# Attention values with the exps as the stationary operand, a ones column for the sums, and x normalised by tokens

## Chip, cores, metric

The kernel runs on one core of one Trainium2 chip. The metric is device time in microseconds (us). A profiled execution gives the span between its first and last instruction, some 3 us (before) below the timed runs. A run is slow when it is over 1.5% above the fastest of the same kernel. The records also give the granted TensorE clock, as a share of full speed, over time.

## The reference, cut to what matters

```python
# q: (8, 16, 384, 64); k, v: (8, 4, 384, 64); four q heads share one k/v head
scores = scale * q @ k.T;  attn = exp(scores - max) / sum;  o = attn @ v
x = o.transpose(0, 2, 1, 3).reshape(8, 384, 1024)          # tokens x (heads * 64)
h = relu(x @ w_in)                                         # 1024 x 1024
u, vv = h[..., :512], h[..., 512:]
vn = (vv - mean(vv)) / sqrt(var(vv) + 1e-6)                # over the 512 features
vs = einsum('ts,bsd->btd', w_spatial, vn) + b_spatial      # mixes the 384 tokens
return (u * vs) @ w_out                                    # 512 x 1024
```

I call the eight batch entries images. Each has 384 tokens in three tiles (t) of 128. The 16 query heads form two groups (gp) of eight, that is, two k/v heads ("half") with four query heads (j) each.

## The kernel before

The program is a hand-written order. Short words stand for steps: `s` a pair of score matmuls, `e` their exps, `m` sums, `r` reciprocal, `x` values, `n` norm, `V` the v half of w_in, `U` the u half, `A` and `H` their first four of eight contraction tiles, `p` spatial, `O` projection. A prime means one image earlier, a plus one image later. Words with `l` load, `c` cast to 16 bits, `t` turn by DMA; `wv` and `wu` load the v and the u half of w_in (index 0: its first four row tiles, 1: its last four), `ws`, `cws`, `tws` load, cast and turn the spatial weights. The steps are played into one queue per engine, and a step that waits holds up what stands behind it in its queue.

The parts that the change touches:

```python
def tiles(dst, quad, streams):                 # four 32-column tiles of the array side by side
    for t, (weights, a) in enumerate(streams):
        for i in range(4):
            half, j = i // 2, quad * 2 + i % 2
            nc.tensor.matmul(dst[32 * i : 32 * (i + 1), :], weights[...],      # 32 stationary columns
                             a[:, half, j * S : (j + 1) * S], ...)             # 384 exps stream
def sums(b, gp, quad):   ...  tiles(f32(x, S), quad, [(ones32, a) for a in parts])
def recip(b, gp, quad):  nc.scalar.activation(rec, sums, AF.Ln); nc.scalar.activation(rec, rec, AF.Exp, scale=-1.0)
def value(b, gp, quad, jj): ... tiles(f32(x, S), quad, [(v16[..., 32 * jj : 32 * (jj + 1)], aT[:, t]) for t in range(NST)])
def norm(b, gp, quad, jj):
    nc.vector.tensor_tensor(T["xT", b][:, gp * 4 + quad * 2 + jj, :], f32(x, S), rec, ALU.mult)
...
def load_w_in(gp, c0, c1):                     # issued by GpSimd, four DMAs of 32 partitions
    for i in range(4): nc.gpsimd.dma_start(w_in16[32 * i : 32 * (i + 1), gp * 4 : gp * 4 + 4, c0:c1], ...)
...
RAMP1 = """ w28 cqjv00 ... w7 cqp011 wv0 cqv010 s0 e0 ... s7 e7
    cv wu0 lk+ lq0+ lq1+ lv+ ws ck+ lk++ cq0+ lq0++ wv1
    s8 m00 r00 x000 n000 ...
    cq1+ wu1 cv+ cws wo ck++ cq0++ m10 ... tws lv++ tk++ tq0++ lq1++ ... """
```

The result of the values stands transposed (features on partitions) and is at once what the feed-forward part needs. VectorE adds the exps of token tiles (`add`, `add2`) to make fewer sums matmuls necessary.

The softmax here doesn't subtract the row's maximum and nothing guards it: scores larger than these inputs give would overflow.

## Time and profile before

| | before |
|---|---|
| time, median of 2 | 252.81 us |
| span of the profiled run | 249.7 us |
| TensorE, VectorE, ScalarE, GpSimd busy | 238.1, 193.9, 172.3, 58.7 us |
| granted clock | 1.00 |

Busy time of TensorE is not work: records of pipelined matmuls overlap (a 512-column matmul of the v half is 380 ns long in the records, and such matmuls start 216 ns apart). What can be read is the distance between starts, and the prediction prices the work by it. Where TensorE never waits, the number of matmuls times that distance is the time.

### The profile page before, as it was taken

Reading aid. Unit: us, or ns where it says so; the run is one execution under the profiler, and the core shown is the slowest. Engines: PE = TensorE matmul, PEld = TensorE weight load, DVE = VectorE, ACT = ScalarE, POOL = GpSimd, SP = SyncE. Lnnn points to the kernel's source line nnn. Section 1 sums busy time; section 2 is a strip of 40 time slices with the busy share of each in tenths; the row PEclk is TensorE's granted clock in tenths of the full one; section 3 lists DMA queues with packets and bytes.
Section 4 is the critical chain, followed back from the end, with each engine's and each line's share of the span. In section 5 each row is a group of like instructions: output and inputs, shape, how many; then the busy total and the mean of one; then the engine's idle time right before and its main releaser. Section 6 shows DMA issues by size and latency. Waiting matters only on the chain.

```text
span 249.7 us, 6046 instructions
## 1 busy us (share of the span) xinstructions
PE 238.1 (95%) x2496; PEld 116.4 (47%) x2496; DVE 193.9 (78%) x365; ACT 172.3 (69%) x229; POOL 58.7 (23%) x100
## 2 busy tenths in 40 slices
PE   7689988989999999999999999999999999999993
PEld 6344434434455444444355444554354444554671
DVE  2626389896979869787979879786979679798853
ACT  3898899987794978677785978677884968430000
POOL 1927960123505400153006400371000000000000
PEclk9999999999999999999999999999999999999999
DMA  6999999749999375967099445959170202110424
GB/s 208 264 270 360 243 200 210 162 90 314 218 295 314 104 83 138 295 181 181 8 253 333 125 76 142 310 161 165 38 213 0 87 0 117 54 59 29 158 97 168
DMA packets 57227, 41.97 MB, mean 168 GB/s; under 512 B 26352, under 2 KB 53360, under 8 KB 57200
## 3 DMA queue, kind: packets, MB, share of 16 engines
q1 hardware_dynamic: 53936, 38.12, 58.2%
q0 software_dynamic: 2848, 3.15, 7.4%
q8 instruction: 19, 0.31, 0.5%
q10 hardware_dynamic: 416, 0.33, 0.4%
q14 instruction: 8, 0.07, 0.1%
HBM read 25.95 MB, written 12.58 MB: 154 GB/s over the span
## 4 chain that ended last, share of the span: by engine, by line
PE 69%; DVE 12%; ACT 12%; issue 3%; DMA 2%; DVEq 0%
PE banks L121 48%; PE banks L337 11%; PE banks L315 10%; ACT aT L327 9%; DVE xT L407 3%; DVE gT L525 2%; DVE sT L350 2%; ACT rec L376 1%; DMA q<-in_q_dram 1%; DVE vs L512 1%; ACT rec L374 1%; DVE bn L467 1%; DMA out_dram<-osb 1%; DVE v_r L456 1%; PE banks L288 1%
## 5 line engine op out<-in xcount | busy, mean ns | idle before, releaser
L327 ACT ACTIVATE aT<-banks 128x1024 f16<-128x1024 f32 x144 | 136.8, 1024 | 33.7 <-PE banks L315 33.5
L315 PE MATMUL banks<-qT,kT 64*128 64x512 f16 x288 | 44.3, 380 | 3.7 <-ACT aT L327 2.1
L121 PE MATMUL banks<-xT,w_in 128*128 128x384 f16 (+1 forms) x320 | 47.0, 294 | 0.6 <-DVE v_r L456 0.6
L121 PE MATMUL banks<-w_out,gT 128*32 128x512 f16 (+2 forms) x496 | 46.3, 379 | 1.3 <-DVE gT L525 0.8
L121 PE MATMUL banks<-w_in,xT 128*128 128x512 f16 x192 | 44.7, 380 | 0.3
L238 POOL CAST q<-q 128x384 f16<-128x384 f32 x57 | 32.2, 598 | 32.0 <-DMA q<-in_q_dram 31.5
L407 DVE TENSOR_TENSOR xT<-banks,rec 128x384 f16<-128x384 f32 x64 | 31.4, 551 | 9.3 <-ACT rec L376 9.2
L121 PEld LDWEIGHTS <-w_in 128*128 128x128 f16 x320 | 27.3, 98 | 16.0 <-issue 1.6
L337 PE MATMUL banks<-aT,v 128*32 128x384 f16 x768 | 34.4, 326 | 0.0
L545 DVE COPY osb<-banks 128x512 f32<-128x512 f32 x46 | 30.2, 683 | 5.4 <-PE banks L121 5.4
L121 PEld LDWEIGHTS <-gT 128*32 128x32 f16 (+1 forms) x496 | 18.4, 96 | 27.4 <-issue 7.2
L121 PEld LDWEIGHTS <-xT 128*128 128x128 f16 x192 | 17.5, 97 | 25.5 <-issue 7.1
L350 DVE TENSOR_TENSOR sT<-aT 128x1024 f16<-128x1024 f16 x39 | 28.1, 734 | 0.0
L337 PEld LDWEIGHTS <-v 128*32 128x32 f16 x768 | 20.6, 97 | 11.0 <-issue 1.2
L195 POOL CAST k<-k 128x768 f16<-128x768 f32 x7 | 6.6, 941 | 78.2 <-DMA k<-in_k_dram 78.2
L454 DVE TENSOR_SCALAR v_r<-banks 128x512 f32<-128x512 f32 x21 | 14.5, 692 | 13.3 <-PE banks L121 12.5
L315 PEld LDWEIGHTS <-kT 64*128 64x128 f16 x288 | 11.3, 94 | 28.6 <-issue 21.9
L374 ACT ACTIVATE rec<-banks 128x384 f32<-128x384 f32 x32 | 15.7, 490 | 8.2 <-PE banks L337 8.1
L121 PE MATMUL banks<-wsT,v_n 128*128 128x384 f16 x96 | 20.5, 327 | 0.1
L512 DVE TENSOR_TENSOR vs<-banks,bias_tp 128x384 f32<-128x384 f32 x28 | 15.3, 550 | 3.6 <-PE banks L121 3.6
L376 ACT ACTIVATE rec<-rec 128x384 f32<-128x384 f32 x32 | 16.7, 523 | 1.0
L467 DVE BATCH_NORM_STATS2 bn<-v_r 128x6 f32<-128x512 f32 x24 | 16.7, 694 | 0.8
(50 smaller groups left out, 144.4 us busy)
## 6 DMA issues: line engine op xcount, KB each, us to landing
q<-in_q_dram SPq DMA_DIRECT2D x31, 384.0 KB, 6.8
out_dram<-osb SPq DMA_DIRECT2D x22, 512.0 KB, 3.2
v<-in_v_dram SPq DMA_DIRECT2D x8, 384.0 KB, 6.9
k<-in_k_dram SPq DMA_DIRECT2D x7, 384.0 KB, 4.8
w_in<-in_moe_w_in_dram POOLq DMA_DIRECT2D x16, 128.0 KB, 6.9
w_out<-in_moe_w_out_dram POOLq DMA_DIRECT2D x2, 512.0 KB, 9.1
out_dram<-osb SPq DMA_DIRECT2D x3, 256.0 KB, 2.0
ws<-in_moe_w_spatial_dram SPq DMA_DIRECT2D x1, 576.0 KB, 9.0
```

The source lines that it names most:

```text
L121: nc.tensor.matmul(dst[c : c + cols], w[:, c : c + cols], m, start=(i == 0), stop=(i == n - 1))
L238: engine(T["q16", b, gp][:, 2 * qd : 2 * qd + 2, :, half, :], T["q32", b, gp][:, qd, 2 * half : 2 * half + 2, :].rearrange("p j (t d) -> p ...
L315: nc.tensor.matmul(banks[:, xs[half], :], T["kT", b][lo:hi, t, gp, :], rhs[lo:hi, c * 512 : (c + 1) * 512], start=True, stop=True,)
L327: nc.scalar.activation(T["aT", b, gp][:, t, :, c * 512 : (c + 1) * 512], banks[:, x : y + 1 : y - x, :], AF.Exp, scale=scale)
L337: nc.tensor.matmul(dst[32 * i : 32 * (i + 1), :], weights if len(weights.shape) == 2 else weights[:, half, :], a[:, half, j * S : (j + 1) ...
L350: engine.tensor_tensor(T["sT", b, gp][:, :, cs], aT[:, 0, :, cs], aT[:, 1, :, cs], ALU.add)
L374: nc.scalar.activation(rec, f32(x, S), AF.Ln)
L376: nc.scalar.activation(rec, rec, AF.Exp, scale=-1.0)
L407: nc.vector.tensor_tensor(T["xT", b][:, gp * 4 + quad * 2 + jj, :], f32(x, S), T["rec", b, gp, quad], ALU.mult)
L467: nc.vector.bn_stats(bn, T["v_r", b, st])
L512: nc.vector.tensor_tensor(vs, f32(x, S), bias_tp, ALU.add)
L545: copy(osb[:, half * 512 : (half + 1) * 512], banks[:, x, :])
```

## The change

The intent: make the exps the stationary operand and v the moving one. A matmul then gives 128 tokens by 64 features. With a ones column appended to v the 65th column is the sum, so the sums matmuls, the VectorE adds, and ScalarE's logarithm and exp for the reciprocal all go. The norm is then one product with a scalar per token and head. In return x stands with tokens on partitions and must be transposed for the feed-forward part. In steady images, two of three token tiles go through TensorE (`Tq`, with a VectorE copy) and one through the DMA (`T`). The whole order was rewritten too (`START`, `STEADY`; in it `X` and `N` are values and norm of one token tile, `Q`, `K` and `Tp` are transposes of q, k and x on TensorE), and w_in is loaded in two DMAs of 128 partitions per piece instead of four of 32.

```diff
-    def tiles(dst, quad, streams): ...      -    def add / add2 / sums / recip ...
+    def value(b, gp, tq):
+        xs = T["X", b, gp, tq] = take2()
+        for half in range(2):
+            for j in range(G):
+                col = column(b, gp, j, tq)
+                aT, o = T["aT", b, gp, col // 4], (col % 4) * P
+                for t in range(NST):
+                    nc.tensor.matmul(banks[:, xs[half], j * (D + 1) : (j + 1) * (D + 1)],
+                                     aT[:, t, half, o : o + P], T["v16", b][:, 2 * gp + half, t, :], ...)
+    def norm(b, gp, tq):
+        nc.vector.reciprocal(rec, ps[:, :, :, D : D + 1])
+        nc.vector.tensor_tensor(T["x16", b, tq][:, gp], ps[:, :, :, 0:D], rec.to_broadcast([P, 2, G, D]), ALU.mult)
+    def turn_x_dma(b, tq): nc.sync.dma_start_transpose(new_xT(b)[:, tq, :, :], ...)
+    def turn_x_all(b, tq, copy): ... 8 x nc.tensor.transpose(...); copy(xT[:, tq, :, :] ..., ps)
... (q by token tiles, load_w_in in two DMAs, the orders) ...
+    START = """ ... s4 wv0 e1 ws e0 wv1 s6 w5 s5 cqv110 lq0+ lv+ cv ckv1 s3 e4 e3 cqv101 ck+ s7 lq1+ K1
+        cq0+ cqv111 wu0 e5 e7 lq0++ lk++ s8 e6 cq1+ Q10 Q11 lq1++ ... s14 e12 cq0++ s16 ...
+        cv+ S1 X12 cws s0+ Q10+ ... s1+ Tp12 H0 wu1 wo e2+ tws V2 ck++ lv++ ... p0 U0 ... """
```

## The prediction

> **What bounds the kernel now.** I first read the engine totals, where TensorE stands out, and then asked whether "busy" means "working", because records of matmuls overlap. In the first fence the columns are busy time, share of the span and instruction count; in the second, the chain of work that ended last in one steady image, they are start, length (both us), what, and how many.
>
> ```profile
> PE 238.1 (95%) x2496; PEld 116.4 (47%) x2496; DVE 193.9 (78%) x365; ACT 172.3 (69%) x229; POOL 58.7 (23%) x100
> ```
>
> ```profile
> 206.60 0.96 PE banks L315 x6
> 207.57 1.84 PE banks L121 x32
> 209.41 2.60 PE banks L337 x64
> 212.01 0.76 PE banks L315 x6
> ```
>
> The chain stays on TensorE here, so the distance between starts is the price of an instruction. 64 column-tiled matmuls of L337 (32 output rows, 384 columns) cost 2.60 us: 40.6 ns each. Six scores run as three concurrent pairs; 0.76 us is three times 216 ns (the start-to-start distance of 512-column matmuls in the trace) and about 0.1 us more. The starts show where that goes: whenever the tiling changes between 64-row, 32-column and whole-array matmuls, the next starts some 95 ns late. A timeline of the last image gives the price of a 128-column matmul with a fresh 128x128 stationary operand:
>
> ```profile
> 234.91 3.74 PE L121 MATMUL banks<-xT,w_in 128*128 128x128 f16 x64
> 238.49 0.81 PE L121 MATMUL banks<-w_out,gT 128*128 128x512 f16 x3
> ```
>
> (238.49-234.91)/64 = 56 ns: the weight load is wholly hidden. 384 columns take 162.5 ns by the same reading. With these prices one steady image is: 36 scores 3.89, v half 24x216 ns = 5.18, u half 32x162.5 ns = 5.20, spatial 12x162.5 ns = 1.95, projection 24x216 ns = 5.18 (the 32-column form of it, 32 in 1.84 us less one switch, costs the same per 128 rows), values 96x40.5 ns = 3.89, sums 24x40.5 ns = 0.97, 12 tiling switches x 95 ns = 1.14. Sum 27.4 us. First scores of successive steady images are 28.02 us apart. So **steady TensorE is 98% real work**, and only some 0.6 us an image is waiting. Over the program the same prices give 229.4 us of the 249.7 us span. The other 20.3 us I place by the stretches between images' first scores (busy time from the windows view, start:end first):
>
> ```profile
> 0.00:6.50 6.50, 5.00 (x53) 4.48 (x54) 1.74 (x9) 2.27 (x3) 0.87 (x7) 1.00 0.72 213
> 6.50:27.40 20.90, 18.00 (x201) 8.03 (x201) 10.77 (x24) 18.71 (x23) 14.34 (x27) 1.00 1.13 292
> 104.50:132.50 28.00, 27.92 (x299) 12.98 (x300) 23.73 (x44) 21.17 (x28) 6.69 (x10) 1.00 0.67 175
> ```
>
> (the numbers after the length are PE, PEld, DVE, ACT, POOL, then granted clock, DMA share, GB/s). Unpriced time is 3.6 us before the first score, 4.9 in image 0, 2.0 and 2.4 in images 1 and 2, 0.5 to 0.7 in each of four steady images, 5.0 in the tail, of which 4.3 us lie after the last matmul's start.
>
> **What the Trainium skill says.** (1) "TensorE: Matmul & The Clock Gate", Back-to-back issue gap: N/2.4 + 2.5 ns when warm. The trace agrees: 55.8 against 56, 162.5 against 162.5, 215.8 against 216. The same section gives 81 ns at N=128 with weight loads; this trace's 56 ns contradicts that. (2) Same page, Weight-path perf modes: a full 128-column non-fp32 stationary operand is loaded by the fast path. No record names the path, but where TensorE has just waited, two 128-column loads start 15 ns apart (44 times), less than a 65-column stream. (3) "TensorEngine Tiling (Array Packing)", Key Properties: a change of tiling mode drains the engine. The 95 ns above agree. (4) "VectorE: DVE Perf Modes", the perf-mode tier table: tensor_tensor with a PSUM operand runs at 1x, a 16-bit copy from PSUM at up to 2x. The trace has 669 ns for a 512-element fp32 add from PSUM and 548 ns for a 768-element fp16 copy, which agree.
>
> **The change, part by part.** What goes and what it cost, by group (busy us, mean ns, then idle before):
>
> ```profile
> L337 PE MATMUL banks<-aT,v 128*32 128x384 f16 x768 | 34.4, 326 | 0.0
> L337 PE MATMUL banks<-aT,ones 128*32 128x384 f16 x128 | 8.5, 328 | 0.0
> L337 PE MATMUL banks<-sT,ones 128*32 128x384 f16 x104 | 7.6, 326 | 0.0
> L350 DVE TENSOR_TENSOR sT<-aT 128x1024 f16<-128x1024 f16 x39 | 28.1, 734 | 0.0
> L356 DVE TENSOR_TENSOR sT<-sT,aT 128x1024 f16<-128x1024 f16 x18 | 13.0, 728 | 0.0
> L374 ACT ACTIVATE rec<-banks 128x384 f32<-128x384 f32 x32 | 15.7, 490 | 8.2 <-PE banks L337 8.1
> L376 ACT ACTIVATE rec<-rec 128x384 f32<-128x384 f32 x32 | 16.7, 523 | 1.0
> L407 DVE TENSOR_TENSOR xT<-banks,rec 128x384 f16<-128x384 f32 x64 | 31.4, 551 | 9.3 <-ACT rec L376 9.2
> ```
>
> TensorE: 1000 column-tiled matmuls go, 1000x40.5 ns = 40.5 us. 1152 matmuls of 65 columns come, each with its own 128x128 load of exps; I price them at 65/2.4+2.5 = 29.6 ns (an estimate from the skill's gap formula, which the three other widths obey), 34.1 us. The built order shows 144 more 128x128 transposes of x, 8.1 us at 56 ns. It also shows 130 tiling switches for 123, +0.7 us, and 41 warm-ups for 44, which lie in idle time. Net **+2.4 us of TensorE work**. In a steady image: values 144x29.6 ns = 4.26, 16 transposes 0.90, 14 switches 1.33 against 3.89+0.97+1.14: 27.9 us, +0.5. That is on the path.
>
> VectorE: it loses 57 adds (41.1 us) and 64 products (64x551 ns = 35.3). It gets 48 products of 512 elements (at 669 ns, the add from PSUM above: 32.1), 48 reciprocals of 8 elements (0.2 us is my estimate, since a 6-element aggregate takes 182 ns: 9.6), and copies of turned x out of PSUM, fifteen of 1024 elements and six of 512 (0.675 and 0.42 us, on the line through 548 ns at 768 and 358 ns at 384: 12.6). Net -22 us. ScalarE: 32x(490+523) ns = -32.4 us. Both lie beside TensorE in the steady part, so there they can only take the 0.6 us of waiting, say 0.3 an image.
>
> The ramp is where they could pay. In image 0 ScalarE works back to back:
>
> ```profile
> 6.97 7.44 ACT L327 ACTIVATE aT<-banks 128x1024 f16<-128x1024 f32 x8 [1.03 <-PE banks L315]
> 14.22 0.57 ACT L374 ACTIVATE rec<-banks 128x384 f32<-128x384 f32 x1
> 14.82 0.52 ACT L376 ACTIVATE rec<-rec 128x384 f32<-128x384 f32 x1
> ```
>
> But the first value matmul needs all nine exps of its head group both before and after (image 0 keeps columns by head, so a token tile meets three column groups). Until about 15.5 us TensorE has only scores and transposes, so most of the 4.9 us stays. The 4.4 us of images 1 and 2 come mostly after that; with less ScalarE and VectorE work and a new order I let them fall to 2. DMA: six 128x1024 x transposes are added, and q loads become fewer and larger; at a share of 0.67 I see no bound.
>
> Sum: 229.4+2.4 = 231.8 of work; waiting 3.6+4.9+2.0+5x0.3+5.0 = 17. Span 248.8 against 249.7, about -1 us; times sit 3.1 us above spans (252.81 against 249.7), so 251.9. Since the new order looks finely interleaved, and orders are made to close gaps, I take another 0.9 us off: **251.0 us**.
>
> **Rivals.** (a) **The short matmuls cost more than 29.6 ns**: two instructions every 30 ns, where the densest stretch now has eight in 162 ns (20 ns each); also the 65-column rows of v start on odd 2-byte places. Each extra ns is 1152 ns: at 35 ns about 257, at 40 ns about 263. For it: nothing this dense ran. Against: the loads' 15 ns distance, and groups within a few ns of each other in the column-tiled quads. (b) **The ramp was ScalarE-bound and opens up**: without reciprocals the 18 exps of image 0 need 18x0.94 = 17 us, not 20, and a lighter VectorE lets image 1 and 2 fill; waiting falls to 12 or 13 us and the time to 247. Against: TensorE's early famine is the exps' own. (c) **A new wait**: the path exps, values, reciprocal, product, transpose, copy, v half is longer than before, and the DMA-turned tile stands in one queue with loads and stores; if it opens a gap of 0.5 us an image, 254 to 255.
>
> **Range and chances.** Between (b) and moderate (a) or (c): 246.5 to 257.5. Over 2% faster needs under 247.75, so nearly all of (b) and the full 29.6: 0.15. Over 2% slower needs above 257.9, so 36 ns or several new gaps: 0.15. Within 2%: 0.70.
>
> **What would show it.** Starts of 65-column matmuls in a group: 29 to 31 ns apart (above 33 and rival (a) holds). First scores of steady images 27.9 to 28.3 us apart. ScalarE busy near 140 us, VectorE near 172, both well below TensorE. The first value matmul not before 15 us. Images 1 and 2 with less waiting than 4.4 us together. What would make me wrong most: the price of the short matmul, then a ramp that the new order fills much better or worse.

## The result

| | before | after |
|---|---|---|
| time, median of 2 | 252.81 us (252.7 to 252.91) | 264.6 us (264.49 to 264.7) |
| span, granted clock | 249.7 us, 1.00 | 262.7 us, 0.974 |
| first score to first score, steady image | 28.02 us | 28.33 us |
| image 0, 1, 2 (first score to next image's first score) | 20.8, 22.4, 26.5 us | 23.8, 34.3, 26.2 us |

The ratio is 1.0466 (95% interval 1.042 to 1.051): the mean time of one kernel's fast runs over that of the other's of the same rounds, so not quite the ratio of medians. The change made the kernel 4.7% slower.

The engine totals of the changed kernel, and its clock row (each digit is a fortieth of the span, in tenths of full speed; 9 is 90% or more):

```profile
PE 246.8 (94%) x2489; PEld 137.3 (52%) x2489; DVE 182.1 (69%) x364; ACT 143.7 (55%) x164; POOL 46.6 (18%) x72
PEclk9979979599999999999999999999999999999999
```

ScalarE fell by 28.6 us and VectorE by 11.8 us, and at most the 1.9 us of steady waiting that went (table below) is time. The clock row has something new: dips in slices 3, 6 and 8. The windows view of the changed kernel, cut at the first scores of images 0, 1, 2, and then one steady image (columns as in the prediction, granted clock third from the end), shows where the time went:

```profile
6.60:30.38 23.78, 20.54 (x256) 12.18 (x256) 14.84 (x36) 17.03 (x18) 9.70 (x14) 0.93 1.00 256
30.38:64.67 34.29, 29.15 (x236) 13.29 (x234) 24.07 (x48) 16.00 (x18) 11.54 (x17) 0.85 0.75 156
119.16:147.49 28.33, 28.33 (x292) 15.60 (x290) 20.56 (x41) 17.62 (x20) 4.89 (x7) 1.00 0.69 184
```

Image 1 takes 34.3 us where its matmuls cost 23.6, at a mean clock of 0.85. The chain of waits of the changed kernel says for what (start, length, what):

```profile
12.90 10.34 DMA q<-in_q_dram
23.25 0.05 issue
23.30 1.60 POOL q L247 x2
24.90 0.66 POOL w_in L137
25.55 9.01 DMA w_in<-in_moe_w_in_dram
34.57 0.05 issue
34.61 2.53 PE banks L113 x6
...
37.89 0.71 POOL w_in L137
38.60 7.36 DMA w_in<-in_moe_w_in_dram
45.95 0.05 issue
46.00 0.82 PE banks L113 x2
```

This is the story in eleven lines. GpSimd waits for image 1's q to land (23.25 us), casts it, and only then issues the next loads of w_in, which land at 34.57; TensorE waits for them in the first partial u product. The last pieces are issued at 37.9 us and land at 45.95; TensorE waits again. Compare GpSimd's queue in the timeline, before (first fence) and after (second):

```profile
10.09 2.14 POOL L148 DMA_DIRECT2D w_in<-in_moe_w_in_dram  x4
25.28 2.17 POOL L148 DMA_DIRECT2D w_in<-in_moe_w_in_dram  x4
28.19 2.04 POOL L168 CAST setup<-ws 128x384 f16<-128x384 f32 x3
```

```profile
24.84 1.43 POOL L137 DMA_DIRECT2D w_in<-in_moe_w_in_dram  x2
32.98 1.60 POOL L247 CAST q<-q 128x768 f16<-128x768 f32 x2 [4.62 <-DMA q<-in_q_dram]
35.33 1.97 POOL L157 CAST setup<-ws 128x384 f16<-128x384 f32 x3
37.89 1.43 POOL L137 DMA_DIRECT2D w_in<-in_moe_w_in_dram  x2
```

The u half of w_in was issued at 10.1 and 25.3 us before, and at 24.8 and 37.9 us after. The spatial weights were cast at 28.2, and now at 35.3 us. Between them stands a cast of *image 2's* q, for which GpSimd waits 4.62 us, though image 2's first score comes only at 64.7 us.

The records of the granted clock are plain: full speed, but half from 14.2 to 17.6, from 34.7 to 38.1 and from 44.9 to 51.7 us. The second begins as TensorE's first wait for w_in ends (33.9 to 34.6 us), the third inside its last one (44.1 to 46.0 us). The profiled run of before had no half clock before its end.

Two groups of the changed kernel that answer to those shown of before:

```profile
L342 PE MATMUL banks<-v,aT 128*128 128x65 f16 x1152 | 45.4, 196 | 0.1
L357 DVE TENSOR_TENSOR x<-banks,rec 128x512 f16<-128x512 f32 x48 | 33.2, 692 | 1.7
```

The price of a short matmul is read from the chain in a stretch without waits:

```profile
83.80 0.76 PE banks L342 x24
```

0.76 us for 24 is 31.7 ns each, and the mean of the distances within groups of images 3 to 7 is 31.7 too; I had priced it at 29.6.

### The profile page after: what moved, and what is told of

Read it like the earlier page. It is cut to its first block, busy times and chain, and to the rows that moved or that the text cites. A ratio compares the mean times of both kernels' runs of the same rounds, so it can differ in the third digit from the quotient of the medians.

```text
span 262.7 us, 5935 instructions
## 1 busy us (share of the span) xinstructions
PE 246.8 (94%) x2489; PEld 137.3 (52%) x2489; DVE 182.1 (69%) x364; ACT 143.7 (55%) x164; POOL 46.6 (18%) x72
## 4 chain that ended last, share of the span: by engine, by line
PE 79%; DMA 12%; DVE 3%; ACT 2%; POOL 1%; issue 1%; SPq 1%; DVEq 0%
PE banks L113 52%; PE banks L342 12%; PE banks L315 12%; DMA w_in<-in_moe_w_in_dram 6%; DMA q<-in_q_dram 5%; PE banks L388 3%; ACT aT L329 2%; DVE v_r L434 1%; POOL q L247 1%; DVE v_n L461 1%; DVE bn L447 1%; POOL w_in L137 1%; SPq L228 0%; DVE osb L525 0%; DVE v_r L436 0%
## 5 line engine op out<-in xcount | busy, mean ns | idle before, releaser
L342 PEld LDWEIGHTS <-aT 128*128 128x128 f16 x1152 | 42.9, 99 | 9.4 <-issue 2.8
L113 PE MATMUL banks<-w_out,gT 128*128 128x512 f16 (+1 forms) x196 | 46.2, 376 | 0.0
L342 PE MATMUL banks<-v,aT 128*128 128x65 f16 x1152 | 45.4, 196 | 0.1
L247 POOL CAST q<-q 128x768 f16<-128x768 f32 (+1 forms) x29 | 23.4, 835 | 91.3 <-DMA q<-in_q_dram 91.3
L357 DVE TENSOR_TENSOR x<-banks,rec 128x512 f16<-128x512 f32 x48 | 33.2, 692 | 1.7
L113 PEld LDWEIGHTS <-xT 128*128 128x128 f16 x192 | 18.1, 99 | 20.7 <-issue 1.1
L113 PEld LDWEIGHTS <-gT 128*128 128x128 f16 x196 | 17.2, 97 | 22.4 <-issue 6.2
L505 DVE SCALAR_TENSOR_TENSOR gT<-banks,vs 128x384 f16<-128x384 f32 x24 | 13.3, 555 | 11.2 <-PE banks L113 11.2
L356 DVE RECIPROCAL rec<-banks 128x8 f32<-128x8 f32 x48 | 9.7, 203 | 10.5 <-PE banks L342 8.7
L113 PEld LDWEIGHTS <-v_n 128*128 128x128 f16 x96 | 8.3, 99 | 10.2 <-DVE v_n L461 3.2
L389 DVE COPY xT<-banks 128x1024 f16<-128x1024 f16 x15 | 10.2, 682 | 4.4 <-PE banks L388 4.4
## 6 DMA issues: line engine op xcount, KB each, us to landing
w_in<-in_moe_w_in_dram POOLq DMA_DIRECT2D x8, 256.0 KB, 7.0
out_dram<-osb SPq DMA_DIRECT2D x3, 256.0 KB, 2.0
```

What stands on the lines that cost most here:

```text
L113: nc.tensor.matmul(dst[c : c + cols], w[:, c : c + cols], m, start=(i == 0), stop=(i == n - 1))
L247: engine(columns(b, gp, T["q16", b, gp])[:, js, :, half, :], T["q32", b, gp][:, half, js, :].rearrange("p j (t d) -> p j t d", t=NST),)
L342: nc.tensor.matmul(banks[:, xs[half], j * (D + 1) : (j + 1) * (D + 1)], aT[:, t, half, o : o + P], T["v16", b][:, 2 * gp + half, t, :], st ...
L357: nc.vector.tensor_tensor(T["x16", b, tq][:, gp], ps[:, :, :, 0:D], rec.to_broadcast([P, 2, G, D]), ALU.mult)
L389: copy(xT[:, tq, :, :].rearrange("p c q -> p (c q)"), ps)
L505: nc.vector.scalar_tensor_tensor(T["gT", b][:, mu, :], src, 0.0, T["vs", b, mu], op0=ALU.max, op1=ALU.mult)
```

## The experiments

The theory after this reading has three parts. **(1)** Late data in image 1: w_in's u half and the spatial weights come late because of where they stand in in-order queues. **(2)** The half clock that follows the waits multiplies them. **(3)** The short matmul costs 31.7 ns, so 2.4 us more. The rival: the new products and the longer path of each image are the loss, and the ramp would be as slow in any order. In all, 12 kernels ran. The kernel before, beside them: its medians were 252.1 to 253.0 us.

### a_wu: the u half of w_in issued early

```diff
-  lv+ cv ckv1 ... cqv111 wu0 e5 ... H0 wu1 wo
+  lv+ cv wu0 wu1 ckv1 ... cqv111 e5 ... H0 wo
```

> The changed kernel with the four loads of the u half of w_in issued right after the first v cast instead of behind GpSimd's casts of later q. Theory (late weights): no matmul waits for w_in at 34.6, 43.6 and 46.0 us any more (2.8 us of idle), the half clock of 34.7 to 38.1 and 44.9 to 51.7 us mostly goes (some 4.5 us), so 257 to 260 us against 264.6. Rival (the short matmuls and the longer path of each image are the loss): under 2 us gained, 263 to 264. Rival (DMA share: 2 MB moved earlier delays the q loads of image 1): wait moves to q casts and it stays at 262 to 266.

Measured: 263.07, 264.24 and 264.79 us, and one run of 400.3 us; ratio of the fast runs 1.046, so **no gain**. A miss, and the third theory of its list came near. The trace that was kept is, unluckily, that of the 400 us run, whose clock was granted at 0.555 from 4.4 us to the end, but for 0.5 between 14.7 and 18.1 us. The TensorE times in it are useless, but the DMA side can be read with care: no matmul waits for w_in. But the q casts of image 1, which wait for their DMA, now start at 28.9 instead of 23.3 us, the spatial weights behind them are cast at 38.1 instead of 35.3 us. I read this as the two megabytes of w_in that were moved forward pushing back what shares the 16 DMA engines with them, and concluded that taking one wait away is not enough: what stands ahead of the needed loads has to be moved back.

### a_cq: image 2's q cast moved behind the weights

```diff
-  e12 cq0++ s16 ... H0 wu1 wo e2+ tws
+  e12 s16 ... H0 wu1 wo cq0++ e2+ tws
```

> The changed kernel with GpSimd's cast of image 2's first q half moved behind the casts of the spatial weights and the last w_in and w_out loads, as in the kernel before. Theory (late weights by GpSimd's order): the spatial weights' transpose and the last w_in piece come 5 to 6 us earlier, so the waits at 42.7 and 46.0 us (3.5 us) and the second stretch of half clock go: 258 to 261 us. The first stretch (34.7 to 38.1) stays. Rival (short matmuls): 263 to 265.

Measured: 258.62 us once, and 268.32, 268.49 and 267.62 us. The one fast run is as expected; three of four were slower than the changed kernel itself. The profiled one (268.32) shows why it was slow. The spatial weights' cast and the last w_in issue did move forward, to 28.8 and 31.6 us. But the spatial weights' DMA transpose, the view of its tile says, took this long from issue to landing:

```profile
L166 SPq DMA_TRANSPOSE wsT<-setup x1: 4272/4272/4272, 30.9 to 30.9; - x1
...
DMA to landing us min/median/max: 19.0/19.0/19.0
```

It took 6.7 us before and 5.3 us in the changed kernel. Here TensorE waited 10.4 us for it, and the last pieces of w_in, issued from 31.6 us, landed at 48.3 and 49.8 us. Between 36 and 44 us the DMA queues moved under 60 GB/s while the transpose of the weights, that of image 2's q and GpSimd's loads of w_in and w_out were in flight together. In the changed kernel's trace the same four overlapped too, without this. Whether they slow each other, and why only in some runs, is not settled by any run here.

### a_fill: idle matmuls where TensorE waits

```diff
-  Tp12 H0 wu1 ... e3+ p0 U0 s12+
+  Tp12 w12 H0 wu1 ... e3+ w25 p0 w40 U0 s12+
```

> The changed kernel with 12 idle matmuls before the first partial u product, 25 before the first spatial product and 40 before the first full u product, all in time that is idle anyway. Nothing arrives earlier, but TensorE is kept busy. If the half clock after the waits costs what it seems (10.2 us at half, of it 9 us busy, so 4.5 us), 259 to 262 us and no half clock between 30 and 55 us. If the clock costs nothing on the path: 264 to 266.

Measured: 261.94, 263.74 and 262.6 us (and a slow 267.35); ratio 1.043 (1.034 to 1.052). The trace did what it was built for: no half clock between 16.2 and 258.5 us, with the data about as late as ever (the first pieces of the u half landed at 34.56 us against 34.57, the last at 45.66 against 45.95). The window of image 1:

```profile
29.92:61.81 31.89, 29.71 (x311) 16.58 (x311) 24.89 (x48) 16.00 (x18) 11.55 (x17) 1.00 0.82 164
```

It took 31.9 instead of 34.3 us. So the half clock's share is about 2.4 us by one trace of each kernel. In the times it is 2.0 us between the medians of the fast runs, and the intervals of the two ratios overlap, so the timed runs alone do not prove it. I had expected 4.5.

### f_ramp: the ramp's loads in order of need

```diff
-  lv+ cv ckv1 ... ck+ s7 ... cqv111 wu0 e5 e7 lq0++ lk++ ... Q11 lq1++ s11 ... e12 cq0++ s16
-  ... X12 cws s0+ ... H0 wu1 wo e2+ tws V2
+  lv+ cv wu0 ckv1 ... ck+ cws s7 ... cqv111 wu1 e5 e7 tws lk++ lq0++ ... Q11 s11 ... e12 s16
+  ... X12 s0+ ... H0 wo lq1++ cq0++ e2+ V2
```

> The changed kernel with the ramp's loads in order of need: the u half of w_in issued early, the spatial weights cast and turned while GpSimd waits for q anyway, the loads and casts of image 2's q and k moved behind them. Nothing else. Theory (late data plus the half clock that follows its waits): image 3 starts some 11 us earlier than in the changed kernel (79 to 81 us against 90.8), clock 0.99 or more, 252 to 255 us. Rival (the short matmuls and the longer path are the loss): no better than 261 us. Moving the u half alone gave 263 to 265, so if the spatial weights' transpose was the rest, this run must show it.

Measured: 258.05 us (257.55 to 259.74, all four fast), ratio 1.024 (1.020 to 1.028). The built programs have the same instructions in the same order on TensorE, VectorE and ScalarE; only loads, casts on GpSimd and one DMA transpose changed their places. The window of image 1:

```profile
31.07:57.94 26.87, 24.97 (x235) 12.22 (x234) 23.52 (x48) 16.00 (x18) 8.28 (x12) 1.00 0.86 197
```

26.9 us at a clock of 1.00, against 34.3 at 0.85. Image 3 starts at 84.1 instead of 90.8 us. So 6.5 of the 11.8 us lost were parts (1) and (2), by medians of different calls; by the loss to before within each call it is 5.9 us, and the traces' spans differ by 6.7. The expected 252 to 255 us was not reached: other costs are left.

### b_late: the same lateness put into the kernel before

```diff
-  cv wu0 lk+ ... lq0++ wv1   /  cq1+ wu1 cv+ cws wo ck++ cq0++
+  cv lk+ ... lq0++ wv1 wu0   /  cq1+ cq0++ cv+ cws wu1 wo ck++
```

> The kernel BEFORE with its loads of the u half of w_in put behind the v half and behind GpSimd's casts of image 2's q and of the spatial weights, as the changed kernel has them; no arithmetic changes. Theory (late weights): the partial u products wait about 4 us at 26 us and the full ones about 3 us at 45 us, plus half clock after: 258 to 264 us. Rival (the new products are the loss, the load order is harmless): 252 to 254.

Measured: 260.92 us (259.71 to 261.82), ratio 1.034 (1.030 to 1.038). The kernel before, with its own products and its own arithmetic, loses 8.8 us from the places of two loads and one cast. Its view of waits has the line that was looked for:

```profile
PE banks L121 <- DMA w_in<-in_moe_w_in_dram: 5.1, 1, 5.1
```

and its clock records have a half from 29.8 to 36.7 us (and one from 12.8 to 16.2 us, as most of these runs have in image 0). Image 0 takes 28.1 instead of 20.8 us. The rival falls for this part: the load order alone costs 8.8 us in a kernel that has none of the new products.

### f_dma2, f_pe3, f_dma3: who turns x

On top of f_ramp, in the steady images: two tiles by DMA (`Tq1` to `T1`), none (`T0` to `Tq0`), or all three (`Tq1`, `Tq2` to `T1`, `T2`; the last image keeps one on TensorE).

> The same with two of three token tiles of x turned by DMA and one by TensorE in images 3 to 6. If the transposes are hidden, steady images take 28.33 - 8 x 0.056 = 27.9 us, four of them 1.8 us less in all than f_ramp. If the DMA queue is the rival's new wait, steady images grow above 28.3.

> The same as f_ramp with all three token tiles turned by TensorE in images 3 to 7. By the prices steady images take 28.33 + 0.45 = 28.8 us, some 2.2 us more than f_ramp in all. If the DMA-turned tile causes a wait, less than that or even fewer us than f_ramp.

> f_ramp with all three token tiles of x turned by DMA in the steady images (the last image keeps one on TensorE). By the prices 28.33 - 0.90 = 27.43 us an image, some 3.6 us less than f_ramp: 254 to 255 us. If the queue of transposes, loads and stores is then too slow, images grow above 27.9.

| x tiles turned by TensorE, of 3 | 3 (f_pe3) | 2 (f_ramp) | 1 (f_dma2) | 0 (f_dma3) |
|---|---|---|---|---|
| steady image, us | 28.77 | 28.33 | 27.88 | 27.43 |
| time, median us | 259.78 | 258.05 | 256.66 | 254.59 |

Each tile on TensorE costs 0.45 us an image, exactly eight transposes at 56 ns. In f_dma3, too, TensorE is busy through the whole steady image, which is only 0.13 us longer than its matmuls at trace prices (the same as in f_ramp), so the DMA's transposes are hidden:

```profile
139.41:166.84 27.43, 27.43 (x274) 14.71 (x274) 19.27 (x39) 17.62 (x20) 4.89 (x7) 1.00 0.84 204
```

The rival of a new wait behind the DMA queue is refuted for steady images. Two of three on TensorE was one choice too cautious for time, with a ramp that is in order.

### a_pad, f_n66 and f_n34: what a short matmul costs

a_pad pads v's rows in the changed kernel to 66 elements; f_n66 and f_n34 are f_ramp with 66 and with 34 columns per value matmul.

```diff
   ... (f_n34; the ones column and the column that the reciprocal reads move to 33)
-  banks[:, xs[half], j * (D + 1) : (j + 1) * (D + 1)],  T["v16", b][:, 2 * gp + half, t, :]
+  banks[:, xs[half], j * (D + 1) : j * (D + 1) + 34],   T["v16", b][:, 2 * gp + half, t, 0:34]
```

> The changed kernel with v's rows padded from 65 to 66 elements, so that every moving operand starts on 4 bytes. If the odd start is what makes the 65-column matmuls 32 ns instead of 29.6, groups of 24 run at 29 to 30 ns a step and the steady images take 28.0 us instead of 28.3: some 2.5 us less, 262 us. If the weight loads or the dispatch are what costs, nothing changes: 264 to 265.

> f_ramp with 66 columns per value matmul, so that operand rows and the sums' places in PSUM start on even elements and the count is even. If the odd count or the odd place (260 bytes) makes 31.7 of 29.6 ns, the distance falls to 30.0 ns and steady images to 28.1 us, some 1.9 us in all. If not, it stays at 31.7 to 32.1 and 258 us.

> A wrong result on purpose: f_ramp with only 34 of the 65 columns of every value matmul (the sums still right, the other dims stale). If the stream of columns sets the pace (65/2.4 + 2.5 = 29.6 ns, some few ns more), matmuls come 25 ns apart or closer and the kernel gains 1152 x 6.7 ns = 7 to 8 us against f_ramp: 250 us. If the load of the 128x128 exps or the dispatch of two instructions sets it (31.7 ns), they stay 30 to 32 ns apart and the time stays at 257 to 258 us.

| columns | 65 (f_ramp, changed kernel) | 65, rows padded (a_pad) | 66 (f_n66) | 34 (f_n34) |
|---|---|---|---|---|
| mean distance in a group, ns | 31.7 | 31.3 | 31.3 | 25.3 |
| steady image, us | 28.33 | 28.27 | 28.27 | 27.40 |
| time, median us | 258.05 (changed: 264.6) | 264.4 | 259.74 | 252.67 |

The chain of f_n34 has 24 of them in 0.60 us, so 25 ns each:

```profile
92.61 0.60 PE banks L342 x24
```

With fewer streamed columns the pace rises, so neither the 128x128 load nor the dispatch of two instructions keeps it at 31.7 ns: a load and a matmul every 30 ns were no limit as such. But 31 columns fewer give back only 6.4 ns, where the trace prices of 128 and 384 columns (56 and 162.5 ns, 0.416 ns a column) give 12.9, and most distances of f_n34 are 25 ns: something else holds it there. Odd starts and the odd count explain little of the extra 2 ns: padding gives back 0.4 ns of it. Single distances at 65 columns run from 29 to 35 ns in a repeating pattern, and what makes them do so stays open. f_n66's image 0 was slow in its profile (26.8 us, with 6.8 us of half clock in two stretches, and TensorE waiting 1.9 us for a q cast), and its time is not below f_ramp's; the steady image is the figure to read.

### f_best: everything that helped

f_dma3 with some 40 idle matmuls between the first scores (`w6 s6`, `w6 s3`, `w6 s7`, `w6 K1`, ...), to keep the clock up in image 0.

> f_dma3 with some 40 idle matmuls between the first scores, where TensorE waits for exps. If the half clock from 13.3 to 16.7 us goes, about 1 us less than f_dma3: 253 to 254 us. If the idle matmuls take banks or delay scores, the same or up to 1 us more.

Measured: 254.13 us (253.91 to 254.98), ratio to before 1.004 (0.996 to 1.012). The clock was 1.00 throughout, and image 0 took 24.3 us as in f_dma3 (24.2 us, whose profiled run happened to have no half clock either). No difference from f_dma3 (254.59 us) can be claimed. So the best version with the new products is **level with the kernel before** and does not beat it; the kernel before remains the fastest by medians (253.0).

## Why the prediction was wrong

The prediction said 251.0 us with a range of 246.5 to 257.5; measured were 264.6. Its sum had three terms, and the profile of the changed kernel can be put beside them. Waiting is the stretch's length less its matmuls at trace prices (31.7 ns for the short ones, in the right two columns), so what a halved clock adds counts as waiting:

| | before | predicted | after | f_ramp |
|---|---|---|---|---|
| TensorE work, us | 229.4 | 231.8 | 234.0 | 234.0 |
| waiting before the first score | 3.6 | 3.6 | 4.1 | 4.1 |
| waiting, image 0 | 4.9 | 4.9 | 6.4 | 7.0 |
| waiting, images 1 and 2 | 4.4 | 2.0 | **12.8** | 5.4 |
| waiting, images 3 to 6 | 2.4 | 1.2 | 0.5 | 0.5 |
| tail | 5.0 | 5.3 | 4.9 | 4.9 |
| span | 249.7 | 248.8 | 262.7 | 256.0 |

("Images 3 to 6" takes four of the five 0.3 us of the prediction's sum; I count the fifth into the tail.)

**The step that failed** is the one that set the waiting of images 1 and 2: "with less ScalarE and VectorE work and a new order I let them fall to 2". It went up from 4.4 to 12.8 us. Two things were wrong in it. The relief did not end the waits that were there: TensorE's idle stretches in these two images of before were 0.8 us behind exps and 1.6 us behind VectorE, in f_ramp they are 0.2 and 2.4 us. And a wait came that before did not have: 2.8 us for w_in and 1.5 us for the turned spatial weights, because the new order put their loads and casts later, with the half clock on top. Beside it stands "DMA: ... at a share of 0.67 I see no bound". 0.67 is the share of a steady image. The windows of the ramp in the same profile had 1.13 and 1.16, and I quoted the first of them without using it. The order of GpSimd's queue of the changed program could be read before any run: a load of the weights behind a cast that waits for q. I counted what moved on TensorE and did not walk the two queues that feed it. f_ramp and b_late show the cause from both sides: putting the loads in order wins some 6 us, putting them out of order in the kernel before costs 8.8 us. The gift of 0.9 us for "orders are made to close gaps" was trust in place of a reading.

**The half clock** was on no list. It needed no long idle time here: TensorE's records have 1.4 and 2.3 us of idle in the 3.4 us before the two stretches of image 1. About 2.4 us, by a_fill's trace, is its share of the 12.8.

**The short matmul** was the right term with the wrong size: 31.7 instead of 29.6 ns, 1152 x 2.1 ns = 2.4 us. Rival (a) in mild form; its reason, two instructions in 30 ns, was wrong (f_n34), and the odd start accounts for 0.4 of the 2.1 ns (a_pad).

**A misreading in image 0.** "The first value matmul needs all nine exps of its head group both before and after" holds only after. In before the first sums start at 13.1 us, with six exps done, and the first values at 13.5; the prediction's own lines show the first reciprocal of these sums at 14.22 us, right behind the eighth exp. After, the first value matmul starts at 15.5 us, behind nine. The wait of image 0 rose from 4.9 to 6.4 us; that the later start is the reason is likely, but no run shows it.

**What held.** The added transposes at 56 ns (0.45 us for a tile, three times over) and the tiling switches held. A steady image rose to 28.33 us, just above the forecast 27.9 to 28.3, by the short matmul (144 x 2.1 ns = 0.3 us), with 0.13 us of waiting: the steady waiting fell as assumed, though no run tells the freed engines from the new order. ScalarE is at 143.7 us (forecast near 140); VectorE at 182.1 is 10 us above the forecast 172, off the path; the reciprocals (203 ns) and copies (682 ns) were as priced, products of 512 cost 692 ns instead of 669. The first value matmul started at 15.5 us, image 0's famine stayed and grew, and rival (b) is dead. Rival (c), a longer path, is refuted in steady images by f_dma2 and f_dma3; a new wait did come, but in the ramp and for weights.

**What stays open.** f_ramp's span is 6.3 us above before: by the table 4.6 us more work and 3.6 us more waiting up to the end of image 2, less 1.9 us in the steady images and 0.1 in the tail (the rest is rounding). I have no run that takes apart the 2.1 us in image 0; 0.8 us of it is, in the trace, a wait of TensorE for GpSimd's cast of image 1's q at 27.6 us, which f_ramp's order made later. Why the DMA queues were so slow in a_cq's profiled run (its other two slow runs have no trace), and why matmuls of 65 columns start 29 to 35 ns apart in turn, is not settled.

## What to carry to other kernels

A change that relieves engines which are not the bound is worth only what waits it ends, so price the added work on the bound engine first: here it was 4.6 us more of matmuls and transposes against 1.9 us of steady waiting. When a change brings a new order, walk every in-order queue, those of loads and casts above all, and ask of each item what stands ahead of it and whether that can wait; read the DMA share in the stretch where the loads happen and not on average. And when TensorE waits a microsecond or two at a time, look at the clock records after it.

## What the Trainium skill lacked or had wrong

- "TensorE: Matmul & The Clock Gate", Back-to-back issue gap: its 81 ns per matmul for N=128 with a weight load each is 56 ns here, also in runs of 64. Its N/2.4 + 2.5 ns holds at 128, 384 and 512 columns, but at 65 columns with a fresh 128x128 operand it gives 29.6 ns where the traces have 31.7 on average, and single distances of 29 to 35. At 34 columns 25.3 ns agree with the floor of about 25 ns in the same page.
- The same page, Part 1 (the HAM clock gate), ties the half clock to an idle window, and its practical rule is to have no idle gaps over about 3 us. It also tells of a kernel whose short idles between groups of matmuls made the clock oscillate, but not how much idle does it. Here half-clock stretches of 3.4 and 6.8 us followed 3.4 us stretches with only 1.4 and 2.3 us of idle in all, no single gap over 1.9 us. Idle matmuls in their place (a_fill) removed them.
- The same page gives clock shares of 4/8, 8/8, 13/16 on a loaded die, and tells of a 1/4 that stuck. One run of a_wu was granted 0.555 for 379 us on a single-core program and took 400.3 us; no page has this share.
- "TensorEngine Tiling (Array Packing)", Key Properties, says that a change of tiling mode drains the engine, but not what it costs: some 95 ns a change, in both directions between 64-row, 32-column and whole-array matmuls.
- "DMA: Bandwidth & Descriptors" has a rule that a transpose next to ordinary DMAs needs nothing. For correctness no run contradicts it. It does not say that a transpose can take 19.0 us to land (a_cq, with other loads and a second transpose in flight) where the same one took 4.2 to 8.3 us in the other 13 traces.
